# Start loads, column order, tile places and the last products of a gated FFT and GeGLU kernel

## The chip, the cores and the metric

The kernel runs on one NeuronCore of a Trainium2 chip. The metric is the device time of one execution, in microseconds (us). Engines are named as in the profile: PE (TensorE: matmuls, with their weight loads as PEld), DVE (VectorE), ACT (ScalarE), POOL (GpSimd) and SP (SyncE, which only issues DMAs here).

## The reference

Two branches on one input, mixed by a gate per token:

```python
# x: 1 x 2048 x 576, w_gate and w_up: 576 x 4608, w_down: 4608 x 576
g = _sigmoid((x * gate_w).sum(-1, keepdims=True))
a = irfft2(rfft2(x) * (w_r + 1j * w_i), s=(2048, 576))
b = (_gelu(x_B @ w_gate) * (x_B @ w_up)) @ w_down
return g * a + (1 - g) * b
```

In the reference B is called with the same x as A. All is float32.

## The kernel before

**Precision and matmuls.** TensorE is used with float32 operands rounded to 12 bits (type fp32r). Each operand is kept as a high and a low part, and a product is three matmuls: high by high, high by low, low by high. The moving operand of the hidden products is 512 columns wide (weights stationary, 128 x 128), that of the down products 288 (half of 576; hidden values stationary).

**Order.** The kernel is one long list of instructions, in an order written out by hand. The 2048 tokens go in two halves (p = 0, 1) of 1024, each in two blocks of 512 (tb). The 4608 hidden features go in 36 tiles of 128 (j). For each half, a few pairs of j are done in the plain way (function `normal`: 2 pairs for p = 0, 6 for p = 1; `chain` makes gate and up products of one j and tb), and the rest with seven products per quadrant in place of eight (class `Block`, function `products`, with `seven` for one of the products; the four results are called c11, c12, c21, c22). Each result passes gelu (ACT), a multiplication (DVE), a copy that rounds to the high part (ACT) and a subtraction for the low part (DVE). The high and low parts stand in a tile taken from a list of free ones (`take`, line 920): the base list is hb0, hb1, hb2 and hx; in the products stage an `extra` list holds the upper half of a gub tile and the tile ext. `wants` says which of them a result prefers.

A down product (`down`, line 958, with `down_mm`, line 930) makes 128 tokens by 576 from two hidden tiles, part 0 and part 1: twelve matmuls of 288 columns into one pdn buffer (two banks of PSUM; there are two such buffers). ACT scales each result into stg (line 975) and POOL adds it to yd in DRAM by a DMA.

**The rest between them.** After each few matmuls stands a call of `gap()`. There, work that was put off by a number of gaps is issued (`at`, `seq`), and then the spectral branch, a generator, goes on by one step: its FFT over rows on DVE, then over columns (`columns`, from line 247) by matmuls with DFT matrices, then back. Each `yield None` in it gives up the rest of that gap; `waits(n)` gives up n gaps. What the generator issues stands in the engines' queues in the place where the gap is.

**Columns.** Sixteen column tiles kb are done in turn, five gaps (g = 0 to 4) for each. At g = 0 stands the forward product of tile kb, `product(0, ...)`, six matmuls of 290 columns into px; the inverse product `product(1, ...)` of the tile before, six into a pdn buffer, is made in `settle()`, either at g = 4 or, when the next thing is the second of a pair of downs (`behind[0]`), at the next g = 0. In that case the two meet. `settle` then also copies the result back to til (ACT) and starts two DMAs of SP (`corner`) that swap two corners of the tile between partition halves; later `corner(..., True)` copies them from a small buffer to their places (ACT). Before the first forward product, the corners of tile 0 are fetched, 7 gaps are given up, the corners are copied, the high part is copied (ACT) and the low part subtracted (DVE, line 292). `load_cc` (POOL) and `load_ww` (SP) load the matrices and filters of coming tiles.

**The start.** From line 1438 on, SP and POOL load five x tiles (256 KB each) and ten weight tiles (128 KB each, for j = 0 and 1, k = 0 to 4) in the order k = 0, 1, 2, 4, 3; six matmuls on a zeroed tile (`idle`, a part of hb2) run meanwhile. ACT and DVE split the loaded tiles, in the same order of k. The first products (`first_chains`, line 879) run over j = 0, 1 for k = 0, 1, 2, and then k = 4 and 3 for each j. A DMA semaphore is used again by the eighth DMA after it, so SP has at most eight DMAs on the way, and POOL too.

**The end.** `finale` (line 1421): the last eight down products go straight to the output. The first four are made one after the other in pdn buffers; for the last four, all part 0 products are made first and then all part 1 products. DVE scales and adds (line 1008), as one instruction for a `pair()` (a whole pdn buffer), or in two halves; each result is stored by a DMA of SP (lines 1010 and 1012).

Of the kernel before, what the change touches and what calls it, by code (L numbers as in the profile page):

```python
# [19 lines left out]
KF = D // 2 + 1  # L20
# [155 lines left out]
def _build(nc, tc, a):  # L176
    with ExitStack() as ctx:
# [5 lines left out]
        def mk(n, shape, dt=F32):  # L183
            return pool.tile([P] + shape, dt, name=n, tag=n)
# [15 lines left out]
        low = mk("low", [5008])  # L200
        ext = mk("ext", [2 * TB])
        raw = [low[:, i * (KT * 256 + D):(i + 1) * (KT * 256 + D)] for i in range(2)]
        hb = [mk(f"hb{i}", [2, TB], F32R) for i in range(3)]
        gl = [mk(f"gl{i}", [TB]) for i in range(2)]
        xraw = mk("xraw", [4, TB])
        stg = [mk(f"stg{i}", [2, HD]) for i in range(4)]
        tmp = mk("tmp", [2 * UNIT + 112])
        sgn = tmp[:, 2 * UNIT + 112 - KF:]
        gs = mk("gs", [NB])
        gate = mk("gate", [NB])  # L210
        omg = mk("omg", [NB])
# [39 lines left out]
        def columns():  # L251
# [39 lines left out]
            def rest_of(l, x, h):  # L291
                vec.tensor_tensor(l, x, f(h), ALU.subtract)
# [38 lines left out]
            load_ww(0)  # L331
            for kb in range(2):
                corner(kb, 0, False)
            yield from waits(7)
            corner(0, 0, True)
            copy(xh2, two(Z[0]))
            yield None
            rest_of(xl2, two(Z[0]), xh2)
            yield None

            def filtered(kb, w):
# [12 lines left out]
            for kb in range(16):  # L354
                was = kb > 0
                z, (w0, w1) = two(Z[kb]), ww[kb % 2]
                zr, zi = z[:, 0], z[:, 1]

                def filter_start():
                    vec.tensor_tensor(zi, v[0][:, :NK], zr, ALU.subtract)  # L360
                    vec.tensor_tensor(zr, v[0][:, :NK], zr, ALU.add)

                def swap():
                    act.activation(vs2[0:64], z[64:128], AF.Copy, scale=-1.0)
                    copy(vs2[64:128], z[0:64])

                def filter_end():
                    vec.tensor_tensor(z, z, two(vs), ALU.add)
                    vec.tensor_tensor(vs2[:, 0], zr, zi, ALU.add)
                    vec.tensor_tensor(vs2[:, 1], zr, zi, ALU.subtract)  # L370

                for g in range(STEP):
                    if g == 0:
                        settle()
                        while kb % 4 == 2 and kb < 14 and made[0] < kb // 4 + 1:
                            credit[0] -= next(side[0]) or 0.0
                        v = product(0, kb, xh, xl)
                        load_ww(kb + 1)
                        corner(kb + 2, 0, False)
                        if was:  # L380
                            copy(yh, vs)
                    elif g == 1:
                        copy(zr, v[1][:, :NK])
                        if kb + 1 < 16:
                            corner(kb + 1, 0, True)
                            copy(xh2, two(Z[kb + 1]))
                        if was:
                            rest_of(yl, vs, yh)
                    elif g == 2:
                        filter_start()  # L390
                    elif g == 3:
                        swap()
                        if kb + 1 < 16:
                            rest_of(xl2, two(Z[kb + 1]), xh2)
                    elif g == 4:
                        vec.tensor_tensor(z, z, two(w0), ALU.mult)
                        vec.tensor_tensor(vs, vs, w1, ALU.mult)
                        filter_end()
                        if was:
                            owed.append(kb - 1)  # L400
                            if not behind[0]:
                                settle()
                        corner(kb - 2, 2, True)
                    credit[0] -= 5.45 / STEP
                    gone[0] = kb * STEP + g
                    yield None
# [167 lines left out]
        def waits(n):  # L574
            for _ in range(n):
                yield None
# [422 lines left out]
        def down_last(prev, t, v, part):  # L999

            i = 4 * prev[2] + t
            whole = len(v) == 1
            down_mm((v[0][:, 0, 0:HD], v[0][:, 1, 0:HD]) if whole else v, prev, t, part, not whole)
            if part == 1:
                o = rest(i).rearrange("p (c k) -> p c k", c=2)
                for c in range(1 if whole else 2):
                    oc, vc = (o, v[0][:, :, 0:HD]) if whole else (o[:, c], v[c])
                    vec.scalar_tensor_tensor(oc, vc, omg[:, 8 + i:9 + i], oc, op0=ALU.mult, op1=ALU.add)
                    if not whole:
                        nc.sync.dma_start(a["y"][8 + i][:, c * HD:(c + 1) * HD], o[:, c])  # L1010
                if whole:
                    nc.sync.dma_start(a["y"][8 + i], rest(i))

# [284 lines left out]
        def products(b, i):  # L1298
# [6 lines left out]
            def finish(name, x, o):  # L1305
                g, v = x
                hold = made[name] = []

                def mult():
                    vec.tensor_tensor(o, o, v, ALU.mult)  # L1310
                    credit[0] -= 0.69

                def gelu():
                    act.activation(o, g, AF.Gelu_apprx_tanh)

                wants = extra if name in ("c21", "c22") else base
                if end and p and name in ("c21", "c12"):
                    gelu()
                    seq((name, p, i), (1, mult), *split_h(o, hold, wants, True))
                else:  # L1320
                    soon = 0 if end else 1
                    high, low = (fn for _, fn in split_h(o, hold, wants))
                    late = name in ("c22", "c12") and not (end and p)
                    seq((name, p, i), (1 + late, gelu), (2 + (soon if name != "c21" else 0) + late, mult), (4 + soon + late - end, high), (5 + 2 * soon + late, low))
# [94 lines left out]
        def finale(pend):  # L1419
# [4 lines left out]
                    down_last(d, t, v, part)  # L1424
                gap()
            d = pend[4][0]
            ps = [pair(), pair(), [ps_one()[:, 0:HD] for _ in range(2)], [ps_gu()[:, 0:HD] for _ in range(2)]]
            for part in range(2):
                for t in range(4):
                    down_last(d, t, ps[t], part)  # L1430
# [3 lines left out]
        x0 = [til[i // 9][:, TB * (i % 9):TB * (i % 9 + 1)] for i in range(2 * KT)]  # L1434
        w0, w1 = (raw[j][:, 0:KT * 256].rearrange("p (t k) -> p t k", t=KT) for j in range(2))
        w0d, w1d = (a["wgu"][j].rearrange("p (t k) -> p t k", t=KT) for j in range(2))
        for k in (0, 1, 2, 4, 3):
            nc.sync.dma_start(x0[k], a["xt"][0][:, k, 0:TB])
            (pl if k else nc.sync).dma_start(w0[:, k], w0d[:, k])
            (pl if k else nc.sync).dma_start(w1[:, k], w1d[:, k])  # L1440
        nc.sync.dma_start(msk, a["msk"])
        for k in range(KT):
            nc.sync.dma_start(x0[5 + k], a["xt"][0][:, k, TB:2 * TB])
        for i in range(2):
# [11 lines left out]
        ps = ps_gu()  # L1456
        for _ in range(6):
            pe.matmul(ps, idle[:, 0:P], idle, start=True, stop=True)
        for k in (0, 1, 2, 4, 3):
            for j, w in ((0, w0), (1, w1)):  # L1460
                g = gu_of(j)
# [160 lines left out]
```

## Time and profile before

| | us |
|---|---|
| median of 3 runs | 1328.49 (1328.35 to 1328.8) |
| profiled execution | 1328.51 |
| its span, first to last instruction | 1326.7 |
| ACT busy | 871.7 (66%) |
| DVE busy | 1162.4 (88%) |

TensorE's granted clock is 1.000 over the span. DMAs move 247.57 MB, 187 GB/s in the mean; by queue, POOL's DMAs take 45.8% of the time of the 16 DMA engines and SP's 34.1%.

How to read the rows: the timeline has start, time, engine, line, operation, "out<-in" by the names of the tiles, and in brackets the idle time of the engine before it and what ended it. A name with buffers leaves the number out: hb is any of hb0, hb1, hb2. "x6" joins six instructions to one row. The time of a PE row goes to the end of its last matmul, which overlaps with the next one. Rows by line (part 5 of the page) have the number of instructions, then busy time in us, the mean of one in ns, and the idle time before them. SPq rows are DMAs issued by SP.

### The profile page before, as it was taken

The numbers are of one execution on the slowest core, as the hardware profiler recorded it, in microseconds if no ns is written. First come the engines' busy times: TensorE is split into PE (matmuls) and PEld (weight loads), VectorE is DVE, ScalarE is ACT, GpSimd is POOL, SyncE is SP. The second block draws the span as 40 slices with busy tenths as digits, with TensorE's granted clock in tenths as the row PEclk, the third lists the DMA queues.
The fourth block names the chain that finished last, engine by engine and source line by source line (L and its number), as shares of the span: only waits on it lengthen the run. The fifth ranks groups of instructions, "written<-read, shape, count | busy, mean of one in ns | idle before, by whom it ended". The sixth has DMA issues, their size and how long they took to land.

```text
span 1326.7 us, 20231 instructions
## 1 busy us (share of the span) xinstructions
PE 1319.0 (99%) x7294; PEld 1166.8 (88%) x7294; DVE 1162.4 (88%) x1653; ACT 871.7 (66%) x1583; POOL 275.6 (21%) x350
## 2 busy tenths in 40 slices
PE   9999999999999999999999999999999999999998
PEld 7888888888888888888888988888888888888897
DVE  7789999978999997976899889799999879999844
ACT  5686765665657556787688888547665686666562
POOL 1011121221212112122302231211222232222331
PEclk9999999999999999999999999999999999999999
DMA  9346777797777777999989998787777897776896
GB/s 353 137 115 128 130 136 136 156 267 164 149 154 137 152 155 183 273 240 283 283 262 235 220 217 195 124 282 190 152 151 147 201 240 153 141 138 126 190 191 176
DMA packets 108693, 247.57 MB, mean 187 GB/s; under 512 B 12848, under 2 KB 17840, under 8 KB 106800
## 3 DMA queue, kind: packets, MB, share of 16 engines
q0 software_dynamic: 46752, 97.34, 45.8%
q1 hardware_dynamic: 61840, 148.93, 34.1%
q8 instruction: 57, 0.93, 0.3%
q14 instruction: 44, 0.36, 0.1%
HBM read 133.88 MB, written 109.95 MB: 184 GB/s over the span
## 4 chain that ended last, share of the span: by engine, by line
PE 94%; issue 3%; DMA 1%; ACT 1%; DVE 1%; POOL 1%; SPq 0%; DVEq 0%; POOLq 0%; ACTq 0%
PE pdn L943 33%; PE pgu L1290 20%; PE px L1290 20%; PE pgu L1292 3%; PE px L1292 3%; PE pgu L859 2%; PE pgu L860 2%; PE pgu L861 2%; PE px L859 1%; PE px L860 1%; PE px L861 1%; PE pdn L304 1%; PE px L304 1%; PE pgu L865 1%; PE pgu L866 1%
## 5 line engine op out<-in xcount | busy, mean ns | idle before, releaser
L956 POOL DMA_DIRECT2D yd<-stg x264 | 226.6, 865 | 941.2 <-ACT stg L975 861.8
L975 ACT ACTIVATE stg<-pdn,omg 128x576 f32<-128x576 f32 x276 | 204.6, 742 | 327.6 <-PE pdn L943 201.9
L943 PE MATMUL pdn<-dn,hb 128*128 128x288 f32 x1572 | 230.9, 294 | 0.1
L943 PEld LDWEIGHTS pdn<-dn,hb 128*128 128x128 f32 x1572 | 221.7, 188 | 9.3 <-ACT stg L975 0.4
L1277 DVE TENSOR_TENSOR gub<-low,gub 128x768 fp32r<-128x768 f32 x124 | 118.0, 952 | 9.6 <-ACT gub L1274 7.0
L1290 PE MATMUL pgu<-xhi,gub 128*128 128x512 f32 x392 | 121.9, 392 | 0.0
L239 ACT ACTIVATE gub<-low 128x512 fp32r<-128x512 f32 (+2 forms) x147 | 97.7, 666 | 19.9 <-DVE low L1267 13.6
L1290 PE MATMUL pgu<-til,gub 128*128 128x512 f32 x420 | 107.5, 391 | 0.0
L943 PE MATMUL pdn<-dn,ext 128*128 128x288 f32 x672 | 106.7, 294 | 0.0
L943 PE MATMUL pdn<-dn,gub 128*128 128x288 f32 x672 | 106.5, 294 | 0.0
L943 PEld LDWEIGHTS pdn<-dn,ext 128*128 128x128 f32 x672 | 98.0, 188 | 4.1
L943 PEld LDWEIGHTS pdn<-dn,gub 128*128 128x128 f32 x672 | 97.9, 188 | 4.0
L1290 PEld LDWEIGHTS pgu<-til,gub 128*128 128x128 f32 x420 | 76.9, 188 | 14.7 <-DVE gub L1277 0.3
L1290 PE MATMUL px<-xhi,gub 128*128 128x512 f32 x280 | 86.9, 392 | 0.0
L1290 PE MATMUL px<-til,gub 128*128 128x512 f32 x336 | 86.0, 391 | 0.0
L943 PE MATMUL pdn<-dn,hx 128*128 128x288 f32 x516 | 82.3, 296 | 0.0
L1290 PEld LDWEIGHTS pgu<-xhi,gub 128*128 128x128 f32 x392 | 70.9, 188 | 12.3
L1267 DVE TENSOR_TENSOR low<-low 128x768 f32<-128x768 f32 x81 | 77.2, 953 | 0.8
L1290 PE MATMUL pgu<-xlo,gub 128*128 128x512 f32 x196 | 76.4, 390 | 0.0
L859 PE MATMUL pgu<-xhi,gub 128*128 128x512 f32 x188 | 73.6, 391 | 0.0
L860 PE MATMUL pgu<-xhi,gub 128*128 128x512 f32 x188 | 73.4, 391 | 0.0
L861 PE MATMUL pgu<-xlo,gub 128*128 128x512 f32 x188 | 73.4, 390 | 0.0
(278 smaller groups left out, 2967.6 us busy)
## 6 DMA issues: line engine op xcount, KB each, us to landing
yd<-stg POOLq DMA_DIRECT2D x264, 288.0 KB, 5.0
low<-ws SPq DMA_DIRECT2D x94, 384.0 KB, 4.9
gub<-wd SPq DMA_DIRECT2D x56, 288.0 KB, 3.9
low<-wgu SPq DMA_DIRECT2D x13, 640.0 KB, 7.3
rows<-col POOLq DMA_DIRECT2D x32, 256.0 KB, 6.3
gub<-ws SPq DMA_DIRECT2D x18, 384.0 KB, 5.8
lo<-dn SPq DMA_DIRECT2D x18, 288.0 KB, 2.9
dn<-lo POOLq DMA_DIRECT2D x18, 288.0 KB, 5.3
```

What stands on the lines that cost most here:

```text
L239: act.activation(o, i, AF.Copy)
L304: pe.matmul(v[al][:, :NK], c[:, al, q], two(x)[:, al], start=n == 0, stop=n == 2)
L859: pe.matmul(ps, w[:, 0, k, c], xhi[tb][:, k], start=k == 0, stop=False)
L860: pe.matmul(ps, w[:, 1, k, c], xhi[tb][:, k], start=False, stop=False)
L861: pe.matmul(ps, w[:, 0, k, c], xlo[tb][:, k], start=False, stop=False)
L943: pe.matmul(ps[half], h[:, l, c], d[:, q, half * HD:(half + 1) * HD], start=part == 0 and n == 0, stop=part == 1 and n == 2)
L956: pl.dma_start(yd[u], o, accum_op=ALU.add)
L975: at(n, lambda: put(u, lambda o: act.activation(o.rearrange("p (c k) -> p c k", c=2), v[:, :, 0:HD], AF.Copy, scale=omg[:, u:u + 1]), i == 0))
L1267: vec.tensor_tensor(o, p, q, ALU.subtract)
L1277: vec.tensor_tensor(w[:, 0:5:2], x, f(w[:, 1:4]), ALU.subtract)
L1290: pe.matmul(ps, l, x[:, t], start=first and t == 0 and q == 0, stop=False, skip_group_check=True)
L1292: pe.matmul(ps, w[:, 512 + P * s:512 + P * (s + 1)], xt, start=False, stop=True, skip_group_check=True)
```

## The change

It has six parts.

- Tiles: hb1 becomes a part, from word 112 on, of a tile of 112 more words, and is allocated after hb2. tmp has 8 words less.
- `columns`: the first corner copy and what follows come one gap sooner; one more gap is given up before the first forward product.
- `columns`, g = 0: `settle()` stands behind the forward product in place of ahead of it.
- `products`: c22 wants the first of the extra tiles (the gub half) alone, c21 the second (ext) alone; before, both wanted either.
- `finale`: the last four down products use px, pgu, a whole pdn buffer and a pdn buffer in halves, in place of two whole pdn buffers, px and pgu. The second half of a result is stored by a DMA that ACT issues.
- The start: SP loads x and weights for k = 0, 1, 2, x of k = 4 and the mask in the order of need. POOL loads only the weights of k = 4 and 3, behind a memset on the warm-up tile, which waits for the six warm-up matmuls.

```diff
-        hb = [mk(f"hb{i}", [2, TB], F32R) for i in range(3)]
+        hb = [mk("hb0", [2, TB], F32R), None, mk("hb2", [2, TB], F32R)]
+        hb[1] = mk("hb1", [2 * TB + 112], F32R)[:, 112:].rearrange("p (l k) -> p l k", l=2)
...
-        tmp = mk("tmp", [2 * UNIT + 112])
-        sgn = tmp[:, 2 * UNIT + 112 - KF:]
+        tmp = mk("tmp", [2 * UNIT + 104])
+        sgn = tmp[:, 2 * UNIT + 104 - KF:]
...
-            yield from waits(7)
+            yield from waits(6)
             corner(0, 0, True)
             copy(xh2, two(Z[0]))
             yield None
             rest_of(xl2, two(Z[0]), xh2)
             yield None
+            yield None
...
                     if g == 0:
-                        settle()
                         while kb % 4 == 2 and kb < 14 and made[0] < kb // 4 + 1:
                             credit[0] -= next(side[0]) or 0.0
                         v = product(0, kb, xh, xl)
+                        settle()
                         load_ww(kb + 1)
                         corner(kb + 2, 0, False)
...
-                        nc.sync.dma_start(a["y"][8 + i][:, c * HD:(c + 1) * HD], o[:, c])
+                        (act if c else nc.sync).dma_start(a["y"][8 + i][:, c * HD:(c + 1) * HD], o[:, c])
...
-                wants = extra if name in ("c21", "c22") else base
+                wants = dict(c21=extra[1:], c22=extra[:1]).get(name, base)
...
-            ps = [pair(), pair(), [ps_one()[:, 0:HD] for _ in range(2)], [ps_gu()[:, 0:HD] for _ in range(2)]]
+            ps = [[ps_one()[:, 0:HD] for _ in range(2)], [ps_gu()[:, 0:HD] for _ in range(2)], pair()]
+            v = ps_dn()
+            ps.append([v[:, c, 0:HD] for c in range(2)])
...
-        for k in (0, 1, 2, 4, 3):
+        for k in (0, 1, 2, 3):
             nc.sync.dma_start(x0[k], a["xt"][0][:, k, 0:TB])
-            (pl if k else nc.sync).dma_start(w0[:, k], w0d[:, k])
-            (pl if k else nc.sync).dma_start(w1[:, k], w1d[:, k])
-        nc.sync.dma_start(msk, a["msk"])
+            if k < 3:
+                nc.sync.dma_start(w0[:, k], w0d[:, k])
+            if k == 2:
+                nc.sync.dma_start(x0[4], a["xt"][0][:, 4, 0:TB])
+            if k < 3:
+                nc.sync.dma_start(w1[:, k], w1d[:, k])
+            if k == 2:
+                nc.sync.dma_start(msk, a["msk"])
...
+        pl.memset(f(idle)[:, 0:16], 0.0)
+        for w, wd, k in ((w0, w0d, 4), (w0, w0d, 3), (w1, w1d, 4), (w1, w1d, 3)):
+            pl.dma_start(w[:, k], wd[:, k])
```

## The prediction

> **What bounds the kernel now.** I read the page first, then busy time by stage (the windows view), then the timeline of TensorE at every place where it waits.
>
> ```profile
> span 1326.7 us, 20231 instructions
> PE 1319.0 (99%) x7294; PEld 1166.8 (88%) x7294; DVE 1162.4 (88%) x1653; ACT 871.7 (66%) x1583; POOL 275.6 (21%) x350
> ...
> 0.00:20.00 20.00, 17.57 (x67) 13.31 (x68) 12.56 (x27) 11.70 (x24) 5.20 (x13) 1.00 0.91 321
> ```
>
> The span is TensorE's own time: 1319.0 of 1326.7 us. The number of matmuls (7294) is not changed. So nothing can be won except where PE waits, at the two ends, and in the few nanoseconds by which one matmul is slower than another. The last row (PE, PEld, DVE, ACT, POOL, clock, DMA share, GB/s) shows that of the few microseconds in which PE is idle, 2.4 lie in the first 20. I list the waits in order of time, as each is met by one part of the change.
>
> The profiled execution took 1328.51 us with its span of 1326.7 us; the median of the three runs is 1328.49 us. The 1.8 us outside the span are taken as fixed, and the sum is made against 1328.5.
>
> **Part 1: the loads at the start.** The 56 matmuls of the first chains (line 879) run from 4.33 to 19.06.
>
> ```profile
> 4.33 1.54 PE L879 MATMUL px<-xhi,gub 128*128 128x512 f32 x4
> 5.71 0.61 PE L879 MATMUL px<-xlo,gub 128*128 128x512 f32 x2
> 6.75 1.19 PE L879 MATMUL pgu<-xhi,gub 128*128 128x512 f32 x4 [0.43 <-ACT gub L239]
> ...
> 8.95 1.20 PE L879 MATMUL px<-xhi,gub 128*128 128x512 f32 x4 [0.55 <-ACT xhi L239]
> ...
> 17.70 1.07 PE L879 MATMUL pgu<-xhi,gub 128*128 128x512 f32 x4
> ...
> 19.06 0.39 PE L859 MATMUL px<-xhi,gub 128*128 128x512 f32 x1
> ...
> 6.28 0.72 ACT L239 ACTIVATE gub<-low 128x256 fp32r<-128x256 f32 x2 [2.01 <-DMA low<-wgu]
> ...
> 8.27 0.63 ACT L239 ACTIVATE xhi<-til 128x512 fp32r<-128x512 f32 x1 [1.26 <-DMA til<-xt]
> ```
>
> The last six (17.70 to 19.06) take 1.36 us, 0.227 each; 56 of them are 12.70, but 14.73 pass. Of the 2.03 lost, the first four matmuls lose 0.47 (1.38 us from 4.33 to 5.71 in place of 0.91); the rest, 1.56, is lost at 6.75 and 8.95, with the refilling behind each. Both waits end with a load: ACT waits for the second weight tile until 6.28 and for the second x tile until 8.27.
>
> ```profile
> 2.12 1.86 SPq L1438 DMA_DIRECT2D til<-xt  x4
> ...
> 2.50:3.00 0.50, 0.50 (x3) 0.40 (x2) 0.00 (x0) 0.00 (x0) 0.50 (x2) 1.00 1.05 397
> 3.50:4.50 1.00, 1.00 (x4) 0.34 (x3) 0.62 (x2) 0.42 (x1) 1.00 (x3) 1.00 0.76 142
> ...
> low<-wgu POOLq DMA_DIRECT2D x8, 128.0 KB, 6.7
> ...
> 10.67 0.62 ACT L239 ACTIVATE xtl<-til 128x512 fp32r<-128x512 f32 x1
> ...
> 12.33 0.49 DVE L243 TENSOR_SCALAR til<-til,msk 128x512 f32<-128x512 f32 x1 [0.77 <-DMA msk<-msk]
> ...
> 12.85 0.75 DVE L244 SCALAR_TENSOR_TENSOR xtl<-xtl,msk,til 128x512 fp32r<-128x512 f32 x1
> ...
> 14.53 1.07 PE L879 MATMUL px<-xtl,gub 128*128 128x512 f32 x4
> ```
>
> Before, eight 128 KB weight loads of POOL run beside SP's. The DMA engines move 397 GB/s at 2.5 to 3.0 and only 142 at 3.5 to 4.5, when POOL's packets have joined, while both late tiles are in the queue. After, SP issues everything for k = 0 to 2 in the order of need, at 0.465 us each (1.86 for four); POOL's four loads (k = 4 and 3) wait, through a memset on the warm-up operand, for the six warm-up matmuls, whose last begins before 4.33. Behind that wait POOL has only these four loads; its zeroing of rows goes ahead. The second weight tile ends 512 KB down SP's queue, the second x tile 768, the third pair of weight tiles 1024. At 397 KB per us from 2.5 us on (some of the first tile is through by then), and with a microsecond allowed for the notice, I estimate that they land near 4.8, 5.4 and 6.1. PE wants their copies at 6.2 (5.71 and two matmuls), 7.5 and 8.9. A microsecond at 142 as before would make each 0.64 later, and ACT's 0.36 and 0.63 us of copies would still fit. So both waits go: **-1.56**.
>
> What is late next? PE is 1.56 us earlier at xtl: 12.97 in place of 14.53. ACT takes the k = 4 weights, then the copy to xtl (0.62), and DVE needs 0.49 + 0.75 behind it: 12.97 - 1.86 - 0.4 gives 10.7 as the last landing that costs nothing. POOL issues that load near 4.6, as the first of four; eight in a row took a median of 6.7 us to landing. At 5 it lands by 9.6; at 6.7 by 11.3, and 0.6 is lost. I take 0 lost, and keep 0 to 0.9. The mask that DVE waited for (0.77) now stands before x tile 3 on SP. Behind all this the SP queue holds the same bytes as before.
>
> **Part 2: first corner copies a gap sooner.**
>
> ```profile
> 657.77 0.68 ACT L239 ACTIVATE dn<-low 128x576 fp32r<-128x576 f32 x1
> ...
> 658.87 0.90 ACT L239 ACTIVATE til<-ext 64x290 f32<-64x290 f32 x2
> ...
> 659.80 0.69 ACT L239 ACTIVATE rows<-til 128x580 fp32r<-128x580 f32 x1
> ...
> 660.52 0.76 DVE L292 TENSOR_TENSOR rows<-til,rows 128x580 fp32r<-128x580 f32 x1 [0.96 <-ACT rows L239]
> ...
> 660.76 1.38 PE L304 MATMUL px<-rows 128*128 128x290 f32 x6
> ```
>
> The six matmuls of the first forward product take 1.38 us, where the one at 785.37 (part 3) takes 0.96: the last two wait for the low part, which DVE ends at 661.28 since ACT's copies end at 660.49. One gap sooner puts the corner copies ahead of the copies to dn (657.77) and hb, about 1.1 us; the low part is then done by 660.2, and PE wants it near 661.0 (661.28 less the 0.3 it idled). The row at 658.87 has no idle time before it, so ACT did not wait for the corner DMAs. The two displaced copies are wanted only by downs after the next chains; ACT's work is the same in sum, so the gelu behind it is not later. **-0.42**; if DVE's queue holds the subtraction back as now, 0.
>
> **Part 3: forward product first.**
>
> ```profile
> 699.57 0.96 PE L943 MATMUL pdn<-dn,hx 128*128 128x288 f32 x6
> ...
> 700.69 1.06 PE L304 MATMUL pdn<-rows 128*128 128x290 f32 x6 [0.16 <-ACT stg L975]
> ...
> 781.64 0.75 DVE L292 TENSOR_TENSOR rows<-til,rows 128x580 fp32r<-128x580 f32 x1
> ...
> 783.05 0.96 PE L943 MATMUL pdn<-dn,hx 128*128 128x288 f32 x6
> ...
> 784.45 1.07 PE L304 MATMUL pdn<-rows 128*128 128x290 f32 x6 [0.45 <-ACT stg L975]
> ...
> 785.37 0.96 PE L304 MATMUL px<-rows 128*128 128x290 f32 x6
> ...
> ACT stg L975 <- PE pdn L943: 16.4, 15, 3.3
> ...
> 1319.08 1.61 PE pdn L943 x12
> ```
>
> The last two rows are of the waits of ACT between 655 and 800 and of the chain of waits near the end: six matmuls of a down step on by 0.80. The two products meet at four places, each right behind two downs. At these two the inverse one waits for ACT to empty a pdn buffer: 700.69 instead of 700.37 (699.57 + 0.80), and 784.45 instead of 783.85; the broken pipeline costs 0.10 and 0.11 more (1.06 and 1.07 against 0.96). That is 0.42 + 0.71. The forward product writes px, and its operands are there (the low part ended at 782.39). Put first, it covers 0.8 us, more than 0.32 and 0.60. On SP the inverse product's corner DMAs keep their place before load_ww; on POOL the two loads behind the products swap, with no other issue between them. The inverse product's copies come 0.8 us later, and their users are ten gaps away. **-1.13**; nothing at the other two places. Bound above: if ACT is relatively later because PE arrives 0.8 us earlier, 0.6 of it returns; but ACT waits for PE 15 times in this stretch, so it moves along.
>
> **Part 4: the last products.**
>
> ```profile
> 1315.36 2.13 PE L943 MATMUL pdn<-dn,hb 128*128 128x288 f32 x12
> ...
> 1316.43 0.83 PEld L943 LDWEIGHTS pdn<-dn,hb 128*128 128x128 f32 x6 [0.35 <-DVE low L1008]
> ...
> 1317.33 0.95 PE L943 MATMUL px<-dn,hb 128*128 128x288 f32 x6
> ...
> 1321.99 1.89 SPq L1010 DMA_DIRECT2D y<-stg  x4
> ...
> 1322.31 0.93 DVE L1008 SCALAR_TENSOR_TENSOR stg<-pgu,omg,stg 128x288 f32<-128x288 f32 x2
> ```
>
> The two pdn products take 1.97 us (1315.36 to 1317.33) against 2 x 0.79 or 0.80: PE waits 0.39 until DVE frees pdn. With px and pgu first, both long free, pdn is wanted 1.6 us later: **-0.39**. DVE takes two halves in 0.93 us (the row of 1322.31) where PE makes a product in 0.80, so it runs a little behind, and ends with the two halves of the last product, as now: its end moves with PE's. The very last store now waits behind SP's previous issue: DVE ends at 1323.24, SP's fourth issue (0.47 each) starts at 1323.41 or later. On ACT, which has nothing queued, it starts 0.06 behind DVE: **-0.15**. No row shows a DMA issued by ACT; between -0.4 (one SP issue) and +0.5 (one issue more), I take SP's price.
>
> **Part 5: the places of the tiles.** hb1 moves 112 words, what is behind it 104 to 112, and the hidden products c22 and c21, which took two tiles in turn, get fixed ones: c22, a down's second operand, the gub half, c21 ext.
>
> ```profile
> L943 PE MATMUL pdn<-dn,hx 128*128 128x288 f32 x516 | 82.3, 296 | 0.0
> ...
> L943 PE MATMUL pdn<-dn,gub 128*128 128x288 f32 x672 | 106.5, 294 | 0.0
> ```
>
> A group of six takes 82.3/86 = 0.957 us with hx, 106.5/112 = 0.951 with gub: 6 ns by the tile alone. From the order and sizes of the tiles (each put at a multiple of 32 bytes, which I assume), hb1 and hx now start a whole number of 4096 bytes behind the gub half; these three are the tiles that hold second operands. If the place makes the difference, 86 groups of hx and as many of hb1 gain 6 ns: **-1.0**. hb1's share can't be seen, since the rows join the three hb tiles. Bounds: -1.6 (the first operands gain half as much) and +0.5 (86 groups lose 6 ns).
>
> [...]
>
> **Sum**: 1.56 + 0.42 + 1.13 + 0.39 + 0.15 + 1.0 = 4.65; 1328.51 - 4.65 = **1323.9 us**, which against the median of the runs (1328.49) is 0.35% less.
>
> **The rivals.**
> *Places don't matter*: part 5 gives 0, the 6 ns of hx belong to its neighbours in the order. 1324.9 us. For it: hx is read in other stages than gub. Against: its mean over 516 matmuls is 296 ns, gub's over 672 is 294.
> *POOL's weights come late*: loads behind a full SP queue; 0.6 to 0.9 us lost at xtl: 1324.5 to 1324.8.
> *Given back*: DVE and ACT don't follow PE, in the stage at 660 to 800, or behind the start (DVE is busy for 88% of the span). Parts 2 and 3 then give a third, the start half: 4.65 - 1.0 - 0.8 = 2.8, and 1.8 with part 5 at 0: 1325.7 to 1326.7. Against: the 15 waits of ACT for PE.
>
> ```profile
> rows<-xn SPq DMA_DIRECT2D x2, 2304.0 KB, 11.9
> ```
>
> *Slower*: POOL's last weight load, issued near 6.3, is served behind SP's long queue. PE wants it at 16.1 (17.70 - 1.56); each microsecond past 15.8 costs one. From a landing at 20.4 the change loses. If it lands with the 2304 KB of rows, near 26, PE waits 10 us: about 1334. Against: in the present trace POOL's loads landed in 6.7 beside a full SP queue.
>
> **How the numbers follow.** Forecast 0.50; places 0.20; late weights 0.14; given back 0.12; slower 0.04. The range takes part 5's two ends, the 0.9 at xtl and most of the third rival: 1322.2 to 1326.5. A measurement tells 0.2%, 2.7 us, from no change; faster by that is below 1325.8: all of the first three and a third of the fourth, less some for steps of a size I have wrong: 0.84. Same 0.12, slower 0.04.
>
> **What would show it.** Right: no PE idle between 4.33 and the first L859 matmul, near 17.5; a first px product of 0.96 us; px before pdn at the meetings with no ACT wait; no PEld wait for DVE near 1315; hx at 0.951 per six. Wrong: PE idle at xtl with ACT waiting for low<-wgu; new waits for ACT stg at 660 to 800; hb or hx slower per six.

## The result and the profile after

The changed kernel takes 1324.29 us (median of 7 runs, 1324.08 to 1325.18), the kernel before 1328.55 (7 runs, 1327.99 to 1328.92). The ratio is 0.997, with an interval of 0.9961 to 0.9979: 4.3 us less. Forecast were 1323.9 us, in a range of 1322.2 to 1326.5.

The page of the profiled execution, which took 1325.16 us, 0.9 more than the median:

```profile
span 1323.4 us, 20232 instructions
PE 1317.2 (100%) x7294; PEld 1166.3 (88%) x7294; DVE 1163.2 (88%) x1654; ACT 871.8 (66%) x1583; POOL 274.5 (21%) x347
...
L945 PE MATMUL pdn<-dn,hb 128*128 128x288 f32 x1572 | 230.3, 294 | 0.0
...
L945 PE MATMUL pdn<-dn,hx 128*128 128x288 f32 x516 | 81.7, 294 | 0.0
```

PE is busy 1.8 us less (1319.0 to 1317.2) and the span is 3.3 us shorter: the rest of the gain was idle time of PE and the ends around it. hx is at 81.7/86 = 0.950 us per six.

The timeline of PE of the same execution, at the places that the change touches:

```profile
659.06 0.97 PE L305 MATMUL px<-rows 128*128 128x290 f32 x6
...
699.25 0.97 PE L305 MATMUL px<-rows 128*128 128x290 f32 x6
700.06 0.97 PE L305 MATMUL pdn<-rows 128*128 128x290 f32 x6
...
782.58 0.97 PE L305 MATMUL px<-rows 128*128 128x290 f32 x6
783.39 0.97 PE L305 MATMUL pdn<-rows 128*128 128x290 f32 x6
...
1312.82 0.97 PE L945 MATMUL px<-dn,hb 128*128 128x288 f32 x6
1313.62 0.96 PE L945 MATMUL pgu<-dn,hb 128*128 128x288 f32 x6
1314.42 1.75 PE L945 MATMUL pdn<-dn,hb 128*128 128x288 f32 x12
1316.01 0.96 PE L945 MATMUL px<-dn,hx 128*128 128x288 f32 x6
```

The first px product takes 0.97 instead of 1.38; at both meetings px stands ahead of pdn and nothing waits for ACT (1.06 and 1.07 are 0.97 now); the two pdn products near the end, the last of part 0, pass in 1.59 (1314.42 to 1316.01) where they took 1.97. So far it went as forecast. But one wait is new:

```profile
678.80 0.43 PE L305 MATMUL px<-rows 128*128 128x290 f32 x2
679.93 0.81 PE L305 MATMUL px<-rows 128*128 128x290 f32 x4 [0.70 <-DVE rows L293]
```

The third matmul of this forward product starts 1.13 us behind the first, where two take 0.27; 0.86 are lost, and 0.11 more as the pipeline fills again (0.64 us from 679.93 to the next product's first matmul, where 0.53 pass at 659). The chain of waits of the same execution (start, duration, what) shows what stands ahead of it. Among 1865 pieces, nearly all of them PE's, is this one:

```profile
626.67 3.16 PE pdn L945 x24
651.43 12.34 DMA til<-away
696.25 3.16 PE pdn L945 x24
```

A transfer that brings back part of the spectral tiles, issued at 651.43, lands 12.34 us later. The timelines of ACT and DVE show how that reaches PE:

```profile
658.67 0.58 ACT L902 ACTIVATE gl<-pgu 128x512 f32<-128x512 f32 x1
663.79 1.27 ACT L137 ACTIVATE xraw<-til 128x580 f32<-128x580 f32 x2 [4.55 <-DMA til<-away]
664.96 0.67 ACT L137 ACTIVATE tmp<-til 128x580 f32<-128x580 f32 x1
665.54 0.39 ACT L240 ACTIVATE til<-px 128x290 f32<-128x290 f32 x1
```
```profile
665.97 0.46 DVE L362 TENSOR_TENSOR til<-px,til 128x290 f32<-128x290 f32 x1 [2.60 <-ACT til L240]
```

The twiddles of the third column tile (L137) stand in ACT's queue ahead of the copies of the column in work (til<-px, whose product had ended at 660 and which ran at 665.54). ACT stood 4.55 us, then DVE 2.60; 14 us later PE had caught up with them. The chain of waits has no piece of PE between the landing at 663.77 and the late matmul at 679.93: it goes through ACT until 670.0 and from there through DVE. Before, ACT stood at the same place, for 2.72 us, and PE did not wait:

```profile
663.70 1.27 ACT L137 ACTIVATE xraw<-til 128x580 f32<-128x580 f32 x2 [2.72 <-DMA til<-away]
```

To find where the time went, I took the start of each matmul in both traces (there are 7294 in each, in an order that differs only at the meetings and in the last products) and subtracted. The table has, for stretches of the trace of before, by how many us a kernel got ahead in them, for all profiled executions. The first stretch counts from the first product's start, at 4.33 in before; up to there the others are ahead by -0.08 to 0.14 us, which is in none of the stretches. "clock" is the time in us at which the trace records TensorE's clock as full, "tail" what lies behind the last of the stretches.

| | clock | 4.3-20 | 20-655 | 655-670 | 670-695 | 695-703 | 703-780 | 780-788 | 788-835 | 835-1314 | 1314-1317 | tail |
|---|---|---|---|---|---|---|---|---|---|---|---|---|
| before | 5.11 | 0 | 0 | 0 | 0 | 0 | 0 | 0 | 0 | 0 | 0 | 0 |
| changed | 6.01 | 1.13 | 0.62 | 0.37 | **-0.96** | 0.41 | -0.27 | 0.73 | -0.10 | 0.65 | 0.39 | 0.41 |
| again | 5.01 | 1.48 | 0.61 | 0.37 | -0.04 | 0.41 | -0.27 | 0.73 | **-0.83** | 0.65 | 0.38 | 0.42 |
| start_only | 5.28 | -0.03 | -0.02 | -0.01 | 0 | -0.02 | -0.01 | 0.02 | 0.01 | 0.03 | 0 | 0.26 |
| cols_only | 5.25 | 0.35 | -0.05 | 0.39 | 0 | 0.41 | -0.01 | 0.71 | -0.01 | 0 | 0 | 0.02 |
| places_only | 4.59 | -0.01 | 0.64 | 0 | -0.04 | -0.01 | -0.26 | 0.08 | -0.09 | 0.65 | 0.01 | 0.10 |
| end_only | 4.47 | -0.62 | -0.06 | -0.01 | 0 | 0.01 | 0 | 0 | 0 | 0.01 | 0.39 | 0.13 |
| no_start | 7.62 | 0.31 | 0.62 | 0.37 | **-1.48** | 0.41 | -0.27 | 0.73 | -0.10 | 0.65 | 0.39 | 0.17 |
| no_cols | 6.96 | 0.70 | 0.63 | 0 | -0.04 | -0.01 | -0.26 | 0.12 | -0.09 | 0.65 | 0.39 | 0.41 |
| no_put | 4.49 | 1.29 | 0.62 | 0.37 | -0.04 | 0.41 | -0.27 | 0.73 | -0.10 | 0.65 | 0.39 | 0.42 |
| away_sooner | 7.17 | 0.56 | 0.64 | **0.06** | -0.04 | 0.41 | -0.27 | 0.73 | -0.10 | 0.65 | 0.38 | 0.42 |
| layout_only | 6.79 | 0.32 | 0.44 | 0 | -0.04 | -0.01 | -0.26 | 0.09 | -0.09 | 0.52 | 0 | 0.07 |
| sp_stores | 7.02 | 0.61 | 0.68 | 0.37 | -0.04 | 0.41 | -0.27 | 0.73 | -0.13 | 0.60 | 0.39 | 0.42 |
| side_later | 7.07 | 0.66 | 0.61 | 0.37 | -0.04 | 0.41 | -0.27 | 0.73 | **-0.80** | 0.60 | 0.39 | 0.42 |

Read down a column: most stretches repeat to 0.05 us wherever their part of the change is in the kernel. Three do not: the start, 655 to 695, and 788 to 835. The experiments are about these.

### The profile page after: what moved, and what is told of

Same layout as the page of the kernel before. It is cut to its first block, busy times and chain, and to the rows that moved or that the text cites. A ratio compares the mean times of both kernels' runs of the same rounds, so it can differ in the third digit from the quotient of the medians.

```text
span 1323.4 us, 20232 instructions
## 1 busy us (share of the span) xinstructions
PE 1317.2 (100%) x7294; PEld 1166.3 (88%) x7294; DVE 1163.2 (88%) x1654; ACT 871.8 (66%) x1583; POOL 274.5 (21%) x347
## 4 chain that ended last, share of the span: by engine, by line
PE 96%; DVE 2%; DMA 1%; ACT 0%; issue 0%; SPq 0%; DVEq 0%; ACTq 0%
PE pdn L945 33%; PE pgu L1292 20%; PE px L1292 20%; PE pgu L1294 3%; PE px L1294 3%; PE pgu L861 3%; PE pgu L862 3%; PE pgu L863 3%; DMA til<-away 1%; PE pdn L305 1%; PE px L305 1%; PE px L861 1%; PE px L862 1%; PE px L863 1%; PE pgu L867 1%; PE pgu L868 1%
## 5 line engine op out<-in xcount | busy, mean ns | idle before, releaser
L945 PEld LDWEIGHTS pdn<-dn,ext 128*128 128x128 f32 x672 | 100.8, 188 | 8.0
L945 PEld LDWEIGHTS pdn<-dn,gub 128*128 128x128 f32 x672 | 95.0, 188 | 0.0
L945 PE MATMUL pdn<-dn,hx 128*128 128x288 f32 x516 | 81.7, 294 | 0.0
```

What stands on the lines that cost most here:

```text
L945: pe.matmul(ps[half], h[:, l, c], d[:, q, half * HD:(half + 1) * HD], start=part == 0 and n == 0, stop=part == 1 and n == 2)
```

## The experiments

The medians are of 5 to 11 runs, beside 10 to 27 of the kernel before on the same chip; the interval of a ratio is 0.0009 to 0.0013 to either side, 1.2 to 1.7 us. The table above tells far smaller things apart, but each row of it is one execution.

### The changed kernel again, and three parts alone

Theory at this point, "landing": TensorE's lead at 660, beyond the slack that ACT had there before, is eaten by a transfer that does not come sooner. Rival, "order": the wait comes of the reordered products. And for the start, which gave 1.08 us up to 10 us instead of 1.56: "clock" against "late loads".

*again* is the changed kernel, with no edit.

> The changed kernel once more. Both theories of the new wait at 680 us and both of the start are read here a second time. Median 1324.3 us. Theory "clock": the start gains 1.5 us at the 20th matmul if TensorE's clock turns full near 5.1 us behind the span's start and 1.1 us if it turns full near 6.0, whichever this execution shows. Rival "late loads": it gains 1.1 us with either clock. Theory "landing": near 680 us TensorE waits again about 1.0 us for DVE's rows, because ACT waits for the second away transfer until its landing near 663.7.

*start_only* has of the change only this:

```diff
-        for k in (0, 1, 2, 4, 3):
+        for k in (0, 1, 2, 3):
             nc.sync.dma_start(x0[k], a["xt"][0][:, k, 0:TB])
-            (pl if k else nc.sync).dma_start(w0[:, k], w0d[:, k])
+            if k < 3:
+                nc.sync.dma_start(w0[:, k], w0d[:, k])
...
+        pl.memset(f(idle)[:, 0:16], 0.0)
```

> The kernel before with the start's loads alone. By the prediction's first step 1326.9 us (1.56 less); by the theory that the clock's turn sets part of it, 1326.9 with a turn near 5.1 us and 1327.4 with one near 6.0. Theory "landing" of the wait near 680 us: TensorE arrives 1.1 to 1.6 us sooner and has 1.2 us of slack against ACT, so that it waits at most 0.4 us near 680, and none of that where the lead is below 1.2. Rival "order" (the wait near 680 comes of the reordered products and the earlier corner copies): no wait of TensorE for rows near 680.

*cols_only*:

```diff
-            yield from waits(7)
+            yield from waits(6)
...
-                        settle()
                         while kb % 4 == 2 and kb < 14 and made[0] < kb // 4 + 1:
                             credit[0] -= next(side[0]) or 0.0
                         v = product(0, kb, xh, xl)
+                        settle()
```

> The kernel before with the corner copies a gap sooner and the forward products first, nothing else. By the prediction's steps 1.55 us less, 1327.0 us. Theory "landing": TensorE's lead is 0.4 us at 660, below the slack of 1.2, so that no wait for rows appears near 680 and all of 0.42 and 1.13 reaches the end. Rival "order": the wait of about 1 us near 680 appears here too, and the gain is 0.6 us or less (1327.9 or more).

*places_only*:

```diff
-        hb = [mk(f"hb{i}", [2, TB], F32R) for i in range(3)]
+        hb = [mk("hb0", [2, TB], F32R), None, mk("hb2", [2, TB], F32R)]
+        hb[1] = mk("hb1", [2 * TB + 112], F32R)[:, 112:].rearrange("p (l k) -> p l k", l=2)
...
-                wants = extra if name in ("c21", "c22") else base
+                wants = dict(c21=extra[1:], c22=extra[:1]).get(name, base)
```

> The kernel before with the tiles' places alone (hb1 and what is behind it, and the fixed tiles of c21 and c22). Theory "places": 1.3 us less (1327.2), 0.65 of it between 100 and 640 us and 0.65 between 835 and 1300, with hx at 0.950 us per six. Rival "places don't matter": 1328.5 and hx at 0.957. Theory "landing": TensorE has a lead of 0.65 us at 660, below the slack of 1.2, so no wait for rows near 680.

Medians: again 1324.48 (ratio 0.9967, 0.9955 to 0.998), start_only 1327.19 (0.9989, 0.9981 to 0.9998), cols_only 1326.76 (0.9986, 0.9977 to 0.9995), places_only 1327.46 (0.9992, 0.9983 to 1.0001); before 1328.67. So 4.19, 1.48, 1.91 and 1.21 us less. (With the end's 0.54, below, the parts alone come to 5.1, but at an uncertainty of 1.2 us or more each this sum of medians shows nothing.)

The columns and the places do in the trace what they did in the changed kernel: 0.39 + 0.41 + 0.71, and 0.64, -0.26, 0.65. The "order" rival falls: cols_only has no wait near 680. But *again* has none either, with a larger lead over the kernel before (2.5 us at 670, where the first trace of the changed kernel had 2.1), and my expectation of it missed: its transfer landed sooner, at 660.7, and ACT stood 1.87 us. In its place stands another wait, in the stretch 788 to 835. ACT and PE of *again*:

```profile
793.86 0.39 ACT L240 ACTIVATE til<-px 128x290 f32<-128x290 f32 x1
795.69 0.90 ACT L240 ACTIVATE til<-ext 64x290 f32<-64x290 f32 x2 [1.44 <-DMA ext<-til]
796.62 0.69 ACT L240 ACTIVATE rows<-til 128x580 fp32r<-128x580 f32 x1
797.22 0.58 ACT L902 ACTIVATE gl<-pgu 128x512 f32<-128x512 f32 x1
```
```profile
797.85 0.50 PE L861 MATMUL pgu<-xhi,gub 128*128 128x512 f32 x1 [0.46 <-ACT gl L902]
```

It is the same figure: an in-order ACT stands at a copy whose DMA (a corner, 8 us on its way) has not landed, a gelu (L902) stands behind it, and PE waits 0.46 us for the pgu buffer that the gelu empties.

The start. In *again* the clock was full at 5.01 us, as in before (5.11), and the gain is 1.48. In *start_only* it was 1.54 by 10 us, counted from the span's start, and then all of it but 0.1 was lost again. PE and ACT of start_only:

```profile
12.08 1.20 PE L879 MATMUL pgu<-xhi,gub 128*128 128x512 f32 x4 [0.30 <-ACT gub L239]
...
14.31 0.47 PE L879 MATMUL px<-xtl,gub 128*128 128x512 f32 x1 [0.57 <-ACT gub L239]
```
```profile
11.61 0.72 ACT L239 ACTIVATE gub<-low 128x256 fp32r<-128x256 f32 x2 [2.05 <-DMA low<-wgu]
```

The load in question is the last weight tile of SP, for k = 2; it landed at 11.59 here, at 10.45 in the changed kernel's trace and at 9.93 in *again*. POOL's four landed between 9.1 and 12.3 in the three.

### The end alone, two parts taken out, and fewer bytes

*end_only*, the kernel before with

```diff
-            ps = [pair(), pair(), [ps_one()[:, 0:HD] for _ in range(2)], [ps_gu()[:, 0:HD] for _ in range(2)]]
+            ps = [[ps_one()[:, 0:HD] for _ in range(2)], [ps_gu()[:, 0:HD] for _ in range(2)], pair()]
+            v = ps_dn()
+            ps.append([v[:, c, 0:HD] for c in range(2)])
...
-                        nc.sync.dma_start(a["y"][8 + i][:, c * HD:(c + 1) * HD], o[:, c])
+                        (act if c else nc.sync).dma_start(a["y"][8 + i][:, c * HD:(c + 1) * HD], o[:, c])
```

> The kernel before with the last products' order and the last stores on ACT's queue alone. By the prediction's fourth step 0.54 us less, against a median before of 1328.6: 1328.1; TensorE's 0.39 near 1315 must go in its trace. If the rest behind TensorE's end is also shorter by 0.4 us, as in the two traces of the changed kernel, 1327.8. With the three parts measured alone (start 1.48, columns 1.91, places 1.21) the four would come to 5.1 to 5.4 us, where all together gave 4.2; rival: this part gains nothing or loses, the four add up to 4.2 and nothing is given back.

*no_start* and *no_cols*, the changed kernel with the first diff above, or the second, taken back:

> The changed kernel without the start's loads. If the parts simply add up, it is slower than the changed kernel by the 1.48 us that the start gave alone: 1325.9. Theory "landing" (the stage of the column products, 650 to 820 us, runs at the DMA engines' rate, and TensorE's lead beyond about 2 us is eaten there by waits of ACT for transfers): without the start the lead at 660 is 0.9 us lower, no wait for rows appears at 680 or 797, and the loss is only 0.4 to 0.8 us: 1324.8 to 1325.2.

> The changed kernel without the sooner corner copies and without the forward products first. If the parts add up: 1.91 us slower than the changed kernel, 1326.3. Theory "landing": the lead at 660 stays near 1.7 to 2.1 us, but from there it has no 1.5 us more, so the wait at 797 does not appear (the one at 680 can): 1325.3 to 1325.9.

*no_put*, the changed kernel with

```diff
-            else:
+            elif wide[0]:
                 pl.dma_start(yd[u], o, accum_op=ALU.add)
```

> The changed kernel without the accumulating stores of the downs in the stage of the column products (288 KB each; these parts of the sum are missing from y), so that the stage moves fewer bytes. Theory "landing": the transfers that ACT waits for land by 1 us or more sooner, the waits of TensorE at 680 and 797 are gone, and the kernel takes 0.8 to 1.0 us less than the changed one: 1323.3 to 1323.5. Rival "own pace" (ACT and DVE are at their own limit there, whatever the transfers do): the waits stay and the time is 1324.3 as before.

Medians: end_only 1328.11 (0.9995, 0.9986 to 1.0003), no_start 1326.0 (0.9979, 0.997 to 0.9988), no_cols 1325.86 (0.9977, 0.9968 to 0.9987), no_put 1323.95 (0.9962, 0.995 to 0.9975); before 1328.65.

*no_start* speaks against my theory as it stood. It is 1.5 us slower than *again*, as if the parts added up, and in its trace PE has a lead of only 1.3 us at 670, and loses more than any other. ACT of no_start:

```profile
665.07 1.27 ACT L137 ACTIVATE xraw<-til 128x580 f32<-128x580 f32 x2 [5.06 <-DMA til<-away]
```

So the lead is not what decides. What does can be read from the rows of L137 in all fourteen traces: ACT stood there 1.71 to 3.65 us in nine, and PE lost nothing; 4.55 us, and PE lost 0.92 (0.96 less the 0.04 of the places); 5.06, and PE lost 1.44. **The loss is ACT's wait less 3.6**, as far as two executions with a loss can tell. In no_put, away_sooner and side_later ACT did not stand there. The second place is alike: at the corner copy near 796 ACT stood 0.20 to 0.73 us in four traces, and PE lost nothing there beyond the 0.10 of the places, or 0.03; 1.39 and 1.44, and it lost 0.70 and 0.73: the wait less 0.7. PE's lead is one term of ACT's wait; the other is how long the transfer takes, and this differs by more: 9.3 to 13.0 us from issue to landing, for the same 580 KB issued at the same gap. *no_cols*, whose median is as expected, was under both bounds (ACT stood 2.75 us).

*no_put* says why they take so long. The DMAs of the stretch 640 to 665, in the changed kernel and in no_put (packets, MB and GB/s, then the transfer in question, with the median time to landing):

```profile
DMA packets 3343, 6.80 MB, mean 272 GB/s; under 512 B 373, under 2 KB 629, under 8 KB 3341
...
til<-away SPq DMA_DIRECT2D x4, 580.0 KB, 8.5
```
```profile
DMA packets 2689, 5.45 MB, mean 218 GB/s; under 512 B 304, under 2 KB 560, under 8 KB 2687
...
til<-away SPq DMA_DIRECT2D x4, 580.0 KB, 4.6
```

By queue, POOL's DMAs take 63.7% of the engines' time for 3.42 MB in the changed kernel and 24.1% for 1.66 MB in no_put, SP's 43.7% for 3.35 MB and 47.4% for 3.76 MB. What the stores add, 39.6% for 1.76 MB, is 1.7 times the time per byte of SP's transfers in the changed kernel. With them away the transfer lands 4.9 us behind its issue, neither wait is there, and the five runs lie within 0.3 us (1323.89 to 1324.19), where those of *again* are spread over 1.7. The median is 0.5 us below that of *again*, which is within the intervals of the two, and 0.3 below the first seven runs of the changed kernel, where 0.8 to 1.0 were expected; an execution in which both transfers are in time loses nothing to begin with.

### Sooner transfers, the tiles alone, the stores on SP

*away_sooner*, the changed kernel with

```diff
-                    for d, n in enumerate((1, 6, 18, 26)):
+                    for d, n in enumerate((1, 6, 14, 26)):
```

> The changed kernel with the two away transfers of the third column tile issued four gaps sooner. In ten profiles so far TensorE's wait near 680 us is 0 where ACT stood up to 3.65 us at that transfer, 0.97 where it stood 4.55 and 1.48 where it stood 5.06: the loss is ACT's wait less 3.6. Theory "issue": the transfer lands by about 5 us sooner, ACT's wait is below 2.5, nothing is lost at 680 in any execution, and the median falls by 0.3 to 0.5 us below the changed kernel's 1324.3 to 1324.5, with a smaller scatter. Rival "bytes": the engines of the DMA are full from 600 to 665, so that the landing stays within 1 us of 660.7 to 665 and the time is the same; or the corner transfers, now behind it, are late in its place.

Median 1325.48 (0.9979, 0.997 to 0.9988), about 1 us more than the changed kernel, at the edge of what the medians can tell. The transfer lands at 650.93 and the wait for it is gone, but what it overtook is late. ACT of away_sooner:

```profile
654.49 0.74 ACT L977 ACTIVATE stg<-pdn,omg 128x576 f32<-128x576 f32 x1 [3.48 <-DMA yd<-stg]
656.40 0.74 ACT L977 ACTIVATE stg<-pdn,omg 128x576 f32<-128x576 f32 x1 [1.17 <-DMA yd<-stg]
657.52 0.90 ACT L240 ACTIVATE til<-ext 64x290 f32<-64x290 f32 x2 [0.38 <-DMA ext<-til]
```

ACT now waits for the stores that free stg, then for the corners, and of the 0.37 of the sooner corner copies 0.06 are left. This is the second half of the rival "bytes" (its first half, a landing near 660.7 to 665, was wrong): in this stretch, where the DMA share is 1.08 (640 to 665 in the changed kernel), the earlier issue only chose which transfer was late. The profiled execution shows 0.3 us of the lost microsecond. Two of its 11 runs took over 1329 us; which transfer was late there, no trace shows.

*layout_only* is *places_only* without the line of `wants`.

> The kernel before with the moved tiles (hb1 and what is behind it) and without the fixed tiles of c21 and c22. All of the change of places together gave 0.64 us by 640, lost 0.3 between 680 and 835 and gave 0.66 from 835 to 1300, the same in each trace. Theory "address": nearly all of it is here, hx at 0.950 per six, 1327.6. Rival "fixed tiles": less than half of the gain up to 640 is here (0.3 or less) and hx stays near 0.957; the loss between 680 and 835, where no c21 or c22 is made, must be here in either case.

Median 1327.82 (0.9993, 0.9984 to 1.0002). hx is at 81.7 us in its page, as in the changed kernel:

```profile
L944 PE MATMUL pdn<-dn,hx 128*128 128x288 f32 x516 | 81.7, 294 | 0.0
```

In the table, 0.44 + 0.52 of 0.64 + 0.65 are its own, and all of the -0.26 and -0.09 between 703 and 835. So it is the place of the tiles: three quarters of the gain, and all of the loss. Why the place matters, no run here shows. That loss is made of nanoseconds as well. From 704 to 779, the 84 matmuls on rows take 0.11 us more in sum and the 112 with xhi 0.19, with the same sums to the nanosecond in both traces of the changed kernel.

*sp_stores*, the changed kernel with the line of the last stores as before:

```diff
-                        (act if c else nc.sync).dma_start(a["y"][8 + i][:, c * HD:(c + 1) * HD], o[:, c])
+                        nc.sync.dma_start(a["y"][8 + i][:, c * HD:(c + 1) * HD], o[:, c])
```

> The changed kernel with all of the last stores on SP, as before. From TensorE's end to the end of the span the six traces with ACT's stores have 4.01 to 4.30 us, the four without 4.17 to 4.43. Theory "queue": the last store waits for SP's issue again, 0.15 to 0.25 us are lost, 4.25 to 4.4 from TensorE's end; medians cannot tell this. Rival "nothing": 4.0 to 4.1, and the shorter end comes of the order of the products.

Median 1324.75 (0.9969, 0.9958 to 0.9981). From PE's end to the span's end it has 4.02 us, the changed kernel 4.03 and 4.01: ACT's queue gives nothing. DMA issues of SP at the end, in sp_stores:

```profile
1316.67 1.80 SPq L1012 DMA_DIRECT2D y<-stg  x4
1318.97 0.33 SPq L1014 DMA_DIRECT2D y<-stg  x1
1319.46 0.82 SPq L1012 DMA_DIRECT2D y<-stg  x2
```

Only two halves are left for the end; SP is free when the first of them comes, and the second begins near 1319.95, 0.09 us behind DVE's end (1319.86); ACT's in the changed kernel began 0.08 behind it (1320.42 and 1320.34).

### The side work later

*side_later*, the changed kernel with

```diff
                 for d in range(1, 4):
-                    yield from tile_twiddles(d, TAKEN, -1, tmps)
+                    yield from waits(3 * (d == 2)); yield from tile_twiddles(d, TAKEN, -1, tmps)
```

> The changed kernel with the twiddles of the third column tile (the three ACT instructions that stood up to 5 us at the away transfer, and what follows them) three gaps later; TensorE's order is the same. Theory "in-order queue": ACT no longer stands at that transfer, the corner copies behind it go at once, and TensorE's wait near 680 us is 0 even in an execution where the transfer lands later than 10 us behind its issue; the median is 1324.0 to 1324.3, the highest run below 1325.2 but for late loads at the start. Rival "the work is only moved": the same 3.5 us of ACT and the DVE work behind them, now behind 669, make the products of 673 to 690 late instead: a wait of TensorE of 0.3 us or more between 670 and 705, and 1324.6 or more.

The order of the column copies and the twiddles on ACT is now the other way round:

```profile
660.57 0.41 ACT L240 ACTIVATE til<-px 128x290 f32<-128x290 f32 x1 [0.82 <-PE px L305]
...
666.18 1.27 ACT L137 ACTIVATE xraw<-til 128x580 f32<-128x580 f32 x2
```

ACT does not stand, PE loses nothing between 655 and 695, and the rival's new wait is not there. The transfer took 10.7 us; by the rule of 3.6 it might have cost nothing in the old order either, so this run shows that the edit is free, not yet what it saves. The other place, which it does not touch, cost 0.70 in this execution, which is the slowest of its runs: 1325.48, where less than 1325.2 was expected. Median 1324.31 (0.9969, 0.9957 to 0.9981): the same as the changed kernel. No version that computes all of y was faster than these two.

## Why the prediction was right

**Start loads, forecast -1.56.** The main step was right: the two tiles, issued by SP at 1.65 and 2.12 as before, landed 1.0 and 2.0 us sooner with POOL's loads out of the way (5.28 and 6.19 in place of 6.26 and 8.24), and both waits ended, in each trace with the new loads but that of no_put. One reading behind it was wrong: the dip to 142 GB/s at 3.5 to 4.5 does not come of POOL's packets. The changed kernel moves 104 GB/s in that microsecond, with SP's packets alone, and what makes the dip is open. The size holds only for the execution that it was read from. "The first four matmuls lose 0.47" was the slow clock until 5.1 us, taken as given; by the trace of PE in two executions, it is not:

```profile
4.31 1.51 PE L881 MATMUL px<-xhi,gub 128*128 128x512 f32 x4
5.66 0.62 PE L881 MATMUL px<-xlo,gub 128*128 128x512 f32 x2
```
```profile
4.28 2.08 PE L881 MATMUL px<-xhi,gub 128*128 128x512 f32 x4
6.15 1.03 PE L881 MATMUL px<-xlo,gub 128*128 128x512 f32 x2
```

The first is *again* (clock full at 5.01 us), the second sp_stores (7.02). With the new loads the gain was 1.48 at 5.01, 1.13 at 6.01, 0.56 to 0.70 at 6.96 to 7.17: in these six traces 0.43 us less for each us (0.92 from 5.01 to 7.17). Where the clock was sooner still (no_put, 4.49), PE waited for the second x tile again, by 0.16 us at 7.61, and the gain was 1.29: about 1.5 is the most that these loads gave in any trace. With the old loads the first 20 us hardly follow the clock (0.32 at 6.79, 0.31 at 7.62, but -0.62 at 4.47, where the second x tile landed at 8.81 and PE waited 1.32 us for it): the waits for loads covered it. The change took that cover away, and the prediction did not ask what would bound the start then. The loads landed near 5.3, 6.2 and 6.9 us where 4.8, 5.4 and 6.1 were estimated, still in time. (The microsecond allowed there for the notice was the author's estimate: in the trace of before the last DMA packet ends at 1325.03 and the last landing is at 1325.39, 0.36 us apart, and 0.39 in the changed kernel.) "What is late next?" named POOL's k = 4 load; what was late was SP's own last weight tile in start_only, which cost all of the gain, and the second x tile in no_put.

In all fourteen traces the clock stays full for 1314.13, 1317.55 or 1320.96 us, in steps of 3.42 and 3.41, and its turn to full is spread over 3.15 us (4.47 to 7.62), with the first matmul at 1.45 or 1.46 in each. What sets the turn, no run shows.

**Sooner corner copies, -0.42**: 0.37 in each trace but away_sooner. **Forward products first, -1.13**: 0.41 + 0.73 = 1.14. **Last products, -0.39**: 0.39.

**The last store on ACT, -0.15**: nothing. The step that failed is "SP's fourth issue (0.47 each) starts at 1323.41 or later": in the new order the last product but one is stored whole, so that there are no four halves in a row at the end, and SP is free. (By the prediction's own rows the step was 0.11 to 0.17; the 0.06 by which ACT was to start behind DVE stands in no row, and in the changed kernel it was 0.08.) The tail is shorter by 0.42 all the same. 0.10 of it lies between PE's end and the last landing (3.09 to 2.99, in *again*); the rest lies behind the last landing, from which it took 1.26 to 1.34 us to the end of the span in the six traces with the old start loads and 1.02 to 1.08 in the eight with the new. Why the start's loads should do that was not tried.

**Places, -1.0**: 0.62 + 0.65 in the two stretches of downs, less 0.04, 0.27 and 0.10 in the columns' stage, 0.86; alone it gave 0.97, the sum of its row from 20 to 1314. The rule held (in layout_only hx is faster by 0.6 us, and the hb tiles by 0.4: 230.9 to 230.5), but that the sum came out near 1.0 is luck: the loss in the other stage, 0.3 to 0.4, was not foreseen, and the fixed tiles of c21 and c22, costed at nothing, gave 0.33. The rival "Places don't matter" falls with layout_only: moved tiles alone gave 0.44 us between 20 and 655. What PE's lost nanoseconds come of, no run here shows.

**Given back, a rival at 0.12**, is, beside the clock at the start, what keeps the sum from being reached, though by another hand: not DVE and ACT at their own pace, but ACT standing in its order at a transfer (4.55 us in the changed kernel, 1.44 in *again*). "ACT waits for PE 15 times, so it moves along" was true for PE's results, and said nothing of what comes by DMA. By the traces the parts that repeat give 0.86 + 0.37 + 1.14 + 0.39 + 0.42 = 3.2 us; the start gives 0.6 to 1.5, and the two waits take 0 to 0.9 of it back. The median of 4.2 to 4.3 lies in that. That the forecast came within 0.4 us of it is in part luck: the tail gave 0.27 more than was forecast, against what the clock and the two waits took. How the timed runs divide it between the clock and the transfers is not known, since only the profiled executions show it.

## What to carry to other kernels

Where a kernel's bound is one engine (here PE, busy for 1319.0 of 1326.7 us), look at its idle gaps one by one: each could be read here to some hundredths of a microsecond from the difference of two traces, stretch by stretch (most repeated to 0.05), long before medians told the parts apart. When a wait goes, ask what it covered: here the turn of the clock at the start (0.43 us less gain for each us that it came later), and transfers that were late all along (ACT stood 2.72 us at one before, and PE did not wait). And a size read from one execution has the scatter of that execution in it; terms that hang on a transfer in a full stretch, or on the start of the clock, deserve a range.

## What was unexpected of the hardware

The same 580 KB transfer, issued in the same place of the order, took 9.3 and 12.3 us in two executions of the changed kernel, and 10.5 in the kernel before, in a stretch where the DMA share is 1.07 to 1.08 (640 to 665). The turn of TensorE's clock lay anywhere between 4.47 and 7.62 us. And the time of a matmul depends, by some nanoseconds and in the same way in each execution, on where in SBUF the tiles lie: 0.957 and 0.950 us per six with hx, and slower, by 0.30 us over 196 matmuls, in the columns' stage, when tiles were moved by 104 to 112 words.
